# Windowed attention and expert routing on one core: gate products, transposes, quotients and loads of the attention stage in another order

## The chip, the cores and the metric

One core of a Trainium2 chip. The metric is the device time of one execution in microseconds (us); three executions of the kernel before gave 659.93 us as their median (659.71 to 661.52).

## The reference

An attention layer feeds a mixture of experts. Shapes: 8 batches, 8 heads, 576 positions, 64 columns a head; then 4608 tokens of 512 columns, 8 experts, hidden width 1024.

```python
scores = scale * np.matmul(q, k.transpose(0, 1, 3, 2))
mask = (rel >= 0) & (rel < window)              # rel = row - column, window = 64
scores = np.where(mask, scores, -1000000000.0)
attn = np.exp(scores - np.max(scores, axis=-1, keepdims=True))
attn = attn / (np.sum(attn, axis=-1, keepdims=True) + 1e-09)
out = np.matmul(attn, v)
...
logits = x @ w_gate                             # x: the attention's output, 4608 x 512
...                                             # tokens go to experts greedily by logit, 576 to each
h = np.maximum(x[mask] @ w1[e], 0.0)
out[mask] = h @ w2[e]
```

## The kernel before

The program has three stretches one behind the other: attention (to about 158 us of the span), the routing of the first expert (to about 185 us), and the experts' two products with the routing of the next expert beside them. The change touches the attention alone.

**Tiling.** A batch has nine blocks of 64 positions. Because of the window a block needs its own keys and those of the block ahead of it, 128 in all. Two consecutive blocks of the whole run (72 of them) make one *unit*: 36 units of 128 rows, 4.5 to a batch. A unit's eight heads are handled in two *groups* of four (`g` = 0, 1).

**A unit's steps.** TensorE multiplies queries and keys (`qk`, L133) into the score banks `Sp`; VectorE adds the mask, negates, and takes the extreme of each row (L142, eight instructions); GpSimd subtracts it (`sm`, L149, one instruction a group); TensorE transposes the result into a bank `Tp` (`tr`, L155, four a group); ScalarE takes the exponent (L157) into `pt`; TensorE multiplies by the values (`pv`, L176) into `Op`. The operand of values has 73 columns a head: 64 of values, 8 that hold the values' product with the gate's weights, and a column of ones that gives the sum of the row. ScalarE copies that sum out (L206), VectorE inverts it (L207) and multiplies the gate columns (L191, into `l`) and the values (L201, into `x`) by it: the *quotient*, once a group. Every fourth unit VectorE sums `l` over heads (L195), and the first expert's choices are then worked off two small operations a unit. `x` is stored to `xs` in memory (L246).

**Order.** The order on every engine is the order in which the code is written; each engine takes its instructions strictly in that order. In loop step `s` stand `qk(s)` with its scores and subtractions, then `tr(s-1)`, then `pv(s-2)` with its quotients, then whatever a table `at` puts at the step's end.

**Gates.** For each batch, in two *halves* (blocks 0 to 3, and 4 to 8), `gate_mm` (L88) multiplies the transposed values `VT` by the gate's weights into a bank `Tp`, `gate_cp` (ScalarE, L92) copies that to `vs`, `gate_tr` (TensorE, L98) transposes it into another bank `Tp`, and `gate_out` (ScalarE, L104 and L107) copies it into the gate columns of `VO`, the values with positions on partitions. `gate_mm` and `gate_cp` stand at the end of one step, `gate_tr` and `gate_out` at the end of the next. There are two `Tp` buffers, handed out in turn to whatever asks: the two groups of `tr`, `gate_mm`, `gate_tr`. A buffer is written again only when ScalarE has read it. Blocks with an even number need values that straddle two tiles of 128 positions; `even` (ScalarE, L119; VectorE, L117, for the first two) moves two halves of 64 partitions into `VE`. These are called *moves* below, two to a block.

**Loads.** The SyncE queue (SP) issues loads in the order written, and waits in that order for the buffers: three each of `Q`, `K` and `VO`, two of `VT`. Batches 0 and 1 are loaded in two parts before the loop, the others by `load_all` (values transposed, queries and keys, values). Stores lag: up to 16 units of `x` are held until step 29.

```python
put(s, gate_mm, b, *i)
put(s, gate_cp, b, *i)
put(s + 1, gate_tr, b, *i)
put(s + 1, gate_out, b, *i)
...
put(s + 1 + max(0, j - 1), even, b, j, not b and j < 2)
```

Of the kernel before, what the change touches and what calls it, by code (L numbers as in the profile page):

```python
# [9 lines left out]
FT = mybir.dt.float32  # L10
# [16 lines left out]
HOLD = 16  # L27
LOADED = 9 * (B - 3) + 12


def attention(ctx, tc, c, q, k, v, vt, gate, xs, L, choices, setup, counters):

    nc = tc.nc
    wgbd, wg = gate
    ld = ctx.enter_context(tc.tile_pool(name="ld", bufs=2))
    wk = ctx.enter_context(tc.tile_pool(name="wk", bufs=3))
    ps = ctx.enter_context(tc.tile_pool(name="ps", bufs=2, space=PSUM))
    po = ctx.enter_context(tc.tile_pool(name="po", bufs=2, space=PSUM))


    SP = [[ps.tile([128, 2, 128], FT, name=f"Sp{r}{i}", bufs=1) for i in range(2)] for r in range(2)]

    def bank():
        return ps.tile([128, 512], FT, name="Tp")
# [1 line left out]
    z = c["zero"]  # L46
    nc.vector.memset(z, 0.0)

    x = po.tile([128, 4, VW], FT, name="Op")
    for _ in range(WARM):  # L50
        nc.tensor.matmul(x[:, 0:2].rearrange("p h w -> p (h w)")[:, 0:128], z, z, start=True, stop=True)
    masks(tc, c)
    Q, K, VO, VE, VT = {}, {}, {}, {}, {}

# [1 line left out]
    PARTS = ((0, 4), (4, NB))  # L56
    ALL = (0, NB)

    def load_vt(b, i0, i1):
        if not i0:  # L60
            VT[b] = ld.tile([128, HP, S], FT, name="VT")
        nc.sync.dma_start(VT[b][:, :, 64 * i0:64 * i1], vt[b, :, :, 64 * i0:64 * i1].rearrange("h p s -> p h s"))

    def load_qk(b, i0, i1, h=slice(0, HP), q2=nc.sync):
        if not i0 and not h.start:
            Q[b] = ld.tile([128, HP, S], FT, name="Q", bufs=3)
            K[b] = ld.tile([128, HP, S], FT, name="K", bufs=3)
        for q1, t, x in ((nc.sync, Q, q), (q2, K, k)):
            q1.dma_start(t[b][:, h, 64 * i0:64 * i1], x[b, h, :, 64 * i0:64 * i1].rearrange("h p s -> p h s"))

    def load_v(b, i0, i1):
        if not i0:
            VO[b] = ld.tile([128, 5, H, VW], FT, name="VO", bufs=3)
        j0, j1 = i0 // 2, i1 // 2
        nc.sync.dma_start(VO[b][:, j0:j1].rearrange("p j h w -> p j (h w)"),
                          v[b, 128 * j0:128 * j1].rearrange("(j p) w -> p j w", p=128))
        if i1 % 2:
            nc.sync.dma_start(VO[b][0:64, j1].rearrange("p h w -> p (h w)"), v[b, 128 * j1:])
# [39 lines left out]
            else:  # L118
                nc.scalar.activation(*a, AF.Copy)  # L119

    PT_, ST, OP_ = {}, {}, {}

    def qk(m, g):
        Sp = [t[g] for t in SP]
# [42 lines left out]
    def pv(m, g):  # L167
        Op = po.tile([128, 4, VW], FT, name="Op")
        pt = PT_.pop((m, g))
# [4 lines left out]
        for h in range(4):  # L174
            for a in range(2):
                nc.tensor.matmul(Op[64 * a:64 * a + 64, h, :], pt[:, h, 64 * a:64 * a + 64],  # L176
                                 vv[a][:, 4 * g + h, :], start=True, stop=True)
        OP_[m, g] = Op

    def norm(m, g):  # L180

        Op = OP_.pop((m, g))
        r = wk.tile([128, 4], FT, name="r", bufs=4)
        if g == 0:
            XT[0] = wk.tile([128, H, D], FT, name="x", bufs=HOLD + 4)
            if m % 4 == 0:
                XT[1] = wk.tile([128, 4, H, E], FT, name="l", bufs=2)
        x, l = XT[0], XT[1]

        def gates():  # L190
            nc.vector.tensor_tensor(l[:, m % 4, 4 * g:4 * g + 4], Op[:, :, 64:72],  # L191
                                    r[:, :, None].to_broadcast([128, 4, E]), OP.mult)
            if g and m in ends:
                j0 = ends[m]
                nc.vector.tensor_reduce(L[:, j0:m + 1, :], l[:, j0 % 4:m % 4 + 1].rearrange("p i h e -> p i e h"),  # L195
                                        axis=AX.X, op=OP.add)
                if m != 34:
                    late.extend(choices(min(j0, 32), m + 1))

        def values():  # L200
            nc.vector.tensor_tensor(x[:, 4 * g:4 * g + 4], Op[:, :, 0:64],  # L201
                                    r[:, :, None].to_broadcast([128, 4, 64]), OP.mult)
            if g:
                stores.append((m, x))

        nc.scalar.activation(r, Op[:, :, 72], AF.Copy, bias=1e-9)  # L206
        return [lambda: nc.vector.reciprocal(r, r), gates, values]  # L207

    for b in range(2):
        for i in PARTS:  # L210
            if b or i[0]:
                load_qk(b, *i)
            else:
                load_qk(b, *i, slice(0, 2), nc.scalar)
                load_qk(b, *i, slice(2, 4), nc.scalar)
                nc.sync.dma_start(wgbd, wg)
                counters()
            load_vt(b, *i)
            load_v(b, *i)

    def load_all(b):
        load_vt(b, *ALL)
        load_qk(b, *ALL)
        load_v(b, *ALL)

    n = 36
    at = {}

    def put(s, f, *a):
        at.setdefault(s, []).append((f, a))  # L230

    for b in range(B):
# [12 lines left out]
    def store(m, x):  # L245
        nc.sync.dma_start(xs[128 * m:128 * m + 128], x.rearrange("p h d -> p (h d)"))  # L246

    def small(s):
        if late:
            late.pop(0)()  # L250
        if s > 1:
            for _ in range(2 if s < 5 else 1):
                next(setup, None)

    for s in range(n + 2):
# [11 lines left out]
        if 2 <= s:  # L267
            for g in range(2):
                pv(s - 2, g)
            nrm = [norm(s - 2, g) for g in range(2)]  # L270
            for inv, gates, values in nrm:
                for f in (inv, gates, values) if s < n + 1 else (inv, gates):
                    f()
            if s >= n:
                while late:
                    late.pop(0)()
            if s == n + 1:
                for inv, gates, values in nrm:
                    values()
        for f, a in at.get(s, []):  # L280
            f(*a)
        for _ in range(1 if 2 * s < LOADED else 2):
            if stores and (len(stores) > HOLD or 2 * s > LOADED):
                store(*stores.pop(0))
    for m, x in stores:
        store(m, x)
# [68 lines left out]
class Routing:  # L355
# [715 lines left out]
```

## Time and profile before

| | |
|---|---|
| median of 3 executions | 659.93 us (659.71 to 661.52) |
| the profiled execution's own time | 659.36 us |
| its span, first to last instruction | 657.7 us |
| mean granted TensorE clock | 0.974 of full speed |
| busy share: TensorE, its weight loads, VectorE, ScalarE, GpSimd | 95%, 81%, 66%, 51%, 33% |
| HBM read and written | 82.15 MB and 18.87 MB |

The busy shares are means over all three stretches, and matmuls are pipelined, so a busy TensorE need not be one at its peak. In rows of single instructions the first number is the start in us from the start of the span, the second the time of the row; "x8" says that eight like instructions were merged; a bracket gives the idle time of that engine ahead of the row and what ended it. "issue" is time in which the engine waited for nothing that the profile shows. PE is TensorE's matmul, PEld its weight load, DVE VectorE, ACT ScalarE, POOL GpSimd, SPq the SyncE queue.

### The profile page before, as it was taken

The page shows a single profiled execution, that of the slowest core. Times are in us where ns is not written, and L with a number is a line of the kernel's source. Part 1 is how long each engine was busy: PE and PEld are TensorE (multiplying, and loading weights), DVE is VectorE, ACT ScalarE, POOL GpSimd, SP SyncE. Part 2 cuts the span into 40 slices and gives each one's busy share as a digit, 9 for nine tenths or more (in the row PEclk, how much of TensorE's full clock was granted, in tenths as well). Part 3 has the DMA queues.
Part 4 walks back from the last instruction along what each step waited for, and adds up shares of the span by engine and source line. Part 5 has one row for each costly group of instructions (what it writes and reads, how often), then busy time and mean ns, then how long its engine had stood idle before and what let it go on. Part 6 is the DMA issues. An engine that isn't in the chain of part 4 may idle for free. (4 is left out here: it accounts for less than half of the span.)

```text
span 657.7 us, 16919 instructions
## 1 busy us (share of the span) xinstructions
PE 622.0 (95%) x6383; PEld 533.8 (81%) x6383; DVE 433.0 (66%) x2109; ACT 335.6 (51%) x602; POOL 219.2 (33%) x233
## 2 busy tenths in 40 slices
PE   7889999996489999999999999999999999999995
PEld 6667777775379878987997898899789879989984
DVE  5788888887787776875886687588668852202300
ACT  2586777783056157436715642672564266256310
POOL 3644545552051043206303320630342063052211
PEclk8999999998589999999999999999999999999998
DMA  9999989931087279739847972975798299939701
GB/s 302 339 366 375 353 286 377 380 142 67 18 279 154 41 266 232 159 106 268 200 87 259 232 164 94 269 197 102 252 223 182 70 289 257 233 106 215 145 24 48
DMA packets 50097, 134.10 MB, mean 204 GB/s; under 512 B 4696, under 2 KB 10968, under 8 KB 50016
## 3 DMA queue, kind: packets, MB, share of 16 engines
q0 software_dynamic: 15280, 52.98, 36.2%
q1 hardware_dynamic: 34192, 79.52, 33.8%
q8 instruction: 50, 0.82, 0.5%
q10 hardware_dynamic: 544, 0.52, 0.2%
q14 instruction: 31, 0.25, 0.1%
HBM read 82.15 MB, written 18.87 MB: 154 GB/s over the span
## 5 line engine op out<-in xcount | busy, mean ns | idle before, releaser
L951 POOL DMA_INDIRECT out<-ot,idx x40 | 40.8, 1021 | 296.4 <-DVE ab L629 98.4
L900 ACT ACTIVATE hh<-h 128x256 fp32r<-128x256 f32 (+1 forms) x128 | 52.1, 408 | 103.7 <-PE h L928 102.7
L971 PE MATMUL o<-wh,hl 128*128 128x512 f32 x256 | 102.2, 399 | 0.0
L971 PE MATMUL o<-wl,hh 128*128 128x512 f32 x256 | 102.0, 398 | 0.0
L971 PE MATMUL o<-wh,hh 128*128 128x512 f32 x256 | 100.4, 392 | 0.0
L149 POOL TENSOR_TENSOR st<-st,mx 128x512 f32<-128x512 f32 x72 | 73.4, 1040 | 73.7 <-DVE mx L142 54.2
L928 PE MATMUL h<-xh,wl 128*128 128x256 f32 (+1 forms) x512 | 94.4, 299 | 0.0
L928 PE MATMUL h<-xh,wh 128*128 128x256 f32 (+1 forms) x512 | 91.6, 299 | 0.7 <-ACT xh L856 0.7
L928 PE MATMUL h<-xl,wh 128*128 128x256 f32 (+1 forms) x512 | 91.1, 297 | 0.5 <-DVE xl L860 0.5
L905 DVE SCALAR_TENSOR_TENSOR hl<-h,hh 128x256 fp32r<-128x256 f32 x128 | 53.3, 416 | 42.4 <-ACT hh L900 42.0
L928 PEld LDWEIGHTS h<-xh,wh 128*128 128x128 f32 x512 | 75.6, 189 | 1.6 <-ACT xh L856 0.8
L928 PEld LDWEIGHTS h<-xh,wl 128*128 128x128 f32 x512 | 76.4, 189 | 0.2
L928 PEld LDWEIGHTS h<-xl,wh 128*128 128x128 f32 x512 | 75.5, 189 | 0.8 <-DVE xl L860 0.7
L142 DVE CUSTOM_DVE_ANT_0 st<-Sp,mask 128x128 f32<-128x128 f32 x288 | 67.4, 285 | 8.0 <-PE Sp L133 7.7
L811 ACT ACTIVATE wh<-st 128x1024 fp32r<-128x1024 f32 x64 | 67.2, 1050 | 3.3 <-DMA st<-w 3.0
L820 ACT ACTIVATE wl<-wh 128x1024 fp32r<-128x1024 f32 x61 | 64.5, 1057 | 1.2
L822 POOL DMA_DIRECT2D wl<-st x61 | 56.9, 1236 | 17.4 <-ACT wl L820 14.5
L971 PEld LDWEIGHTS o<-wl,hh 128*128 128x128 f32 x256 | 48.1, 188 | 9.3
L971 PEld LDWEIGHTS o<-wh,hh 128*128 128x128 f32 x256 | 48.2, 188 | 9.2
L971 PEld LDWEIGHTS o<-wh,hl 128*128 128x128 f32 x256 | 48.3, 189 | 8.8
L860 DVE TENSOR_TENSOR xl<-tp,xh 128x512 fp32r<-128x512 f32 (+1 forms) x40 | 25.0, 633 | 45.3 <-ACT xh L856 44.9
L866 POOL DMA_INDIRECT xg<-xs,idx x40 | 40.8, 1020 | 34.7 <-DVE eq L709 23.1
(178 smaller groups left out, 1088.4 us busy)
## 6 DMA issues: line engine op xcount, KB each, us to landing
wl<-st POOLq DMA_DIRECT2D x61, 512.0 KB
st<-w SPq DMA_DIRECT2D x60, 512.0 KB, 10.0
xs<-x SPq DMA_DIRECT2D x36, 256.0 KB, 8.0
VO<-v SPq DMA_DIRECT2D x6, 1168.0 KB, 17.8
VT<-vt SPq DMA_DIRECT2D x6, 1152.0 KB, 14.3
Q<-q SPq DMA_DIRECT2D x6, 1152.0 KB
K<-k SPq DMA_DIRECT2D x6, 1152.0 KB
VO<-v SPq DMA_DIRECT2D x4, 584.0 KB, 11.1
```

The lines of the kernel that those rows point to most:

```text
L142: nc.vector.tensor_tensor_reduce(st[:, h, :], Sp[h % 2][:, h // 2], mk, scale=-0.125, scalar=3.0e38, op0=OP.add, op1=OP.min, accum_out=mx[ ...
L149: nc.gpsimd.tensor_tensor(st, st, mx[:, :, None].to_broadcast([128, 4, 128]), OP.subtract)
L811: nc.scalar.activation(hi, st[i], AF.Copy)
L820: nc.scalar.activation(lo, hi.bitcast(FT), AF.Copy, scale=-1.0)
L822: nc.gpsimd.dma_start(lo.bitcast(FT), st[i], accum_op=OP.add)
L860: nc.vector.tensor_tensor(xl[:, :, r], t[:, :, :n], xh[:, :, r].bitcast(FT), OP.subtract)
L866: nc.gpsimd.indirect_dma_start(out=g[0:n, a], out_offset=None, in_=self.xs, in_offset=IndirectOffsetOnAxis(ap=idx[0:n, a:a + 1], axis=0))
L900: nc.scalar.activation(hh[:, f, c0:c1], h, AF.Relu)
L905: nc.vector.scalar_tensor_tensor(t, h[:, a - c0:b - c0], 0.0, hh[:, f, a:b].bitcast(FT), op0=OP.max, op1=OP.subtract)
L928: nc.tensor.matmul(h, wv[:, cc, 128 * (f % 2):128 * (f % 2) + 128], xt[:, cc, c0:c1], start=(k == 0), stop=(k == 11))
L951: nc.gpsimd.indirect_dma_start(out=self.out, out_offset=IndirectOffsetOnAxis(ap=idx[0:m, a:a + 1], axis=0), in_=ot[0:m], in_offset=None)
L971: nc.tensor.matmul(o, ht[:, f, 128 * a:128 * a + 128], wt[:, 512 * (f % 2):512 * (f % 2) + 512], start=(k == 0), stop=(k == 23))
```

## The change

- **Banks.** `Sp` becomes one tile of two banks for each group, `Op` one tile of two banks for both groups, in one copy in place of two of one bank each. The banks in use stay eight.
- **One quotient a unit.** The copy of the sums, the inversion, and the two multiplications each handle both groups: four instructions a unit where there were eight, and they begin when the second group's products are done.
- **Gates.** `gate_tr` and `gate_out` move from the end of the next step to between its `qk` and its `tr`. The moves come at a step's end behind `gate_mm` and `gate_cp`. The halves come in the last step of the batch before and the first of their own (the first two batches and the last have steps of their own).
- **Loads.** Of batch 0, blocks 4 and 5 of queries and keys come ahead of the values; of batches from 2 on, queries and keys, then transposed values, then (a step later) values.
- **The end.** In step 36 the products and quotient of unit 34 stand ahead of the transposes of unit 35, in the banks of the scores' first group.
- `LOADED`, from which two stores are allowed a step, is step 30 in place of 29.

```diff
-LOADED = 9 * (B - 3) + 12
+LOADED = 29
...
-    po = ctx.enter_context(tc.tile_pool(name="po", bufs=2, space=PSUM))
+    po = ctx.enter_context(tc.tile_pool(name="po", bufs=1, space=PSUM))
...
+    SB = [ps.tile([128, 2, 512], FT, name=f"Sp{i}", bufs=1) for i in range(2)]
+    SP = [[x[:, r, 0:256].rearrange("p (h k) -> p h k", h=2) for x in SB] for r in range(2)]
...
+    def pv(m):
+        Ob = SB[0] if m == n - 2 else po.tile([128, 2, 512], FT, name="Op")
+        Op = Ob[:, :, 0:4 * VW].rearrange("p g (h w) -> p g h w", h=4)
...
+        def values():
+            nc.vector.tensor_tensor(x, Op[:, :, :, 0:64], r[:, :, :, None].to_broadcast([128, 2, 4, 64]), OP.mult)
+            stores.append((m, x.rearrange("p g h d -> p (g h d)")))
+
+        nc.scalar.activation(r, Op[:, :, :, 72], AF.Copy, bias=1e-9)
+        return lambda: nc.vector.reciprocal(r, r), gates, values
...
+    load_qk(0, 4, 6)
+    load_vt(0, 0, 4)
+    load_v(0, 0, 4)
+    load_qk(0, 6, NB)
+    load_vt(0, 4, NB)
+    load_v(0, 4, NB)
...
-        s0 = (9 * (b - 1) + (6 if b < 4 else 7)) // 2
-        for i, s in zip(PARTS, ((0, 2), (3, 5))[b] if b < 2 else (s0, s0 + 2)):
+        f = 9 * b // 2
+        for i, s in zip(PARTS, {0: (1, 2), 1: (5, 6), B - 1: (f - 3, f - 1)}.get(b, (f - 1, f))):
             put(s, gate_mm, b, *i)
             put(s, gate_cp, b, *i)
-            put(s + 1, gate_tr, b, *i)
-            put(s + 1, gate_out, b, *i)
+            put(s + 0.5, gate_tr, b, *i)
+            put(s + 0.5, gate_out, b, *i)
             for j in range(4):
                 if i[0] <= 2 * j + 2 < i[1]:
-                    put(s + 1 + max(0, j - 1), even, b, j, not b and j < 2)
+                    put(s + 1.25 + max(0, j - 1), even, b, j, not b and j < 2)
     for b in range(2, B):
-        put((9 * (b - 2) + 5) // 2, load_all, b)
+        f = 9 * b // 2
+        put(f - 7, load_qk, b, *ALL)
+        put(f - 7, load_vt, b, *ALL)
+        put(f - 6, load_v, b, *ALL)
...
+        do(s - 0.5)
+        if s == n:
+            quotients(s)
         if 1 <= s < n + 1:
             for g in range(2):
                 tr(s - 1, g)
...
+        if 2 <= s and s != n:
+            quotients(s)
+        do(s)
+        do(s + 0.25)
```

ScalarE's order around the second half of batch 5, before (`vs` is the copy of a gate product, `VO<-Tp` the copy into the gate columns, `VE` the moves, `pt` the exponents, `r` the sums):

```order
L92 ACTIVATE vs<-Tp 128x320
L157 ACTIVATE pt<-Tp 128x512 x2
L206 ACTIVATE r<-Op 128x4 x2
L104 ACTIVATE VO<-Tp 128x16x8
L107 ACTIVATE VO<-Tp 64x8x8
L119 ACTIVATE VE<-VO 64x584 x2
L157 ACTIVATE pt<-Tp 128x512 x2
```

and with the change:

```order
L93 ACTIVATE vs<-Tp 128x320
L120 ACTIVATE VE<-VO 64x584 x2
L105 ACTIVATE VO<-Tp 128x16x8
L108 ACTIVATE VO<-Tp 64x8x8
L159 ACTIVATE pt<-Tp 128x512 x2
L206 ACTIVATE r<-Op 128x8
```

The copy into the gate columns stood a unit behind the copy of the product, ahead of the moves; now it stands in the same stretch with a pair of moves between the two. Of the sixteen halves, four had moves between the two copies; now twelve have, one of them (second half of batch 2) four instructions.

TensorE's order at the same place, with the change (`Sp` scores, `Tp<-ident,vs` the gate's transposes, `Tp<-ident,st` a unit's eight transposes, `Op` products; before, the gate's transposes stood behind the unit's products, a whole unit's `qk` ahead of the next `Tp<-ident,st`):

```order
L89 MATMUL Tp<-VT,wgs 32x320 x4
L135 MATMUL Sp_95<-K,Q 64x128 x8
L135 MATMUL Sp_96<-K,Q 64x128 x8
L99 MATMUL Tp<-ident,vs 128x128 x2
L99 MATMUL Tp<-ident,vs 64x128
L157 MATMUL Tp<-ident,st 128x128 x8
L180 MATMUL Op<-VE,pt 64x73
```

The gate's transposes now stand directly ahead of a unit's transposes. Since the two `Tp` buffers are handed out in turn, the gate's product and the first group's transposes share one, the gate's transposes and the second group's transposes the other.

## Rows read from the trace of the kernel before

**Rows 1.** Busy time of each engine in two stretches, the attention up to unit 11 and from there to the last scores: us, length, busy us and instructions of PE, PEld, DVE, ACT, POOL, granted clock, DMA share, GB/s.

```profile
5.00:54.00 49.00, 42.40 (x782) 32.49 (x783) 35.73 (x260) 27.19 (x65) 24.10 (x25) 0.97 1.06 359
54.00:147.00 93.00, 90.86 (x1838) 72.05 (x1837) 79.25 (x568) 70.19 (x165) 48.36 (x48) 1.00 0.88 318
```

**Rows 2.** Groups of instructions up to 165 us, shapes apart: line, engine, operation, tiles, shapes, count | busy us, mean ns of one | idle us ahead of them and what ended it.

```profile
L119 ACT ACTIVATE VE<-VO 64x584 f32<-64x584 f32 x60 | 41.3, 689 | 1.3
...
L201 DVE TENSOR_TENSOR x<-Op,r 128x256 f32<-128x256 f32 x72 | 29.8, 415 | 0.2 <-issue 0.2
...
L191 DVE TENSOR_TENSOR l<-Op,r 128x32 f32<-128x32 f32 x72 | 13.8, 192 | 7.5
```

**Rows 3.** Single instructions in order of time, end of unit 18 and unit 19, which has no gate product: scores, transposes, products on PE, the second group's quotient on DVE and the next scores.

```profile
84.71 0.44 PE L98 MATMUL Tp<-ident,vs 128*128 128x128 f32 x2
...
85.08 1.10 PE L133 MATMUL Sp<-K,Q 64*64 64x128 f32 x32
...
85.24 0.17 DVE L207 RECIPROCAL r<-r 128x4 f32<-128x4 f32 x1
...
85.51 0.19 DVE L191 TENSOR_TENSOR l<-Op,r 128x32 f32<-128x32 f32 x1
85.62 0.41 DVE L201 TENSOR_TENSOR x<-Op,r 128x256 f32<-128x256 f32 x1
85.95 0.28 DVE L142 CUSTOM_DVE_ANT_0 st<-Sp,mask 128x128 f32<-128x128 f32 x1
86.11 1.09 PE L155 MATMUL Tp<-ident,st 128*128 128x128 f32 x8
...
87.14 0.28 PE L176 MATMUL Op<-VE,pt 128*64 128x73 f32 x1
```

**Rows 4.** Single instructions of PE and of ACT, one gate half of five blocks: its product, the scores behind it, its transposes; the copy of the product, the two copies into the gate columns; and a pair of moves.

```profile
88.31 0.74 PE L88 MATMUL Tp<-VT,wgs 128*32 128x320 f32 x8
88.99 1.10 PE L133 MATMUL Sp<-K,Q 64*64 64x128 f32 x32
...
92.22 0.55 PE L98 MATMUL Tp<-ident,vs 128*128 128x128 f32 x3
92.70 0.56 PE L133 MATMUL Sp<-K,Q 64*64 64x128 f32 x12
...
85.51 1.39 ACT L119 ACTIVATE VE<-VO 64x584 f32<-64x584 f32 x2
...
89.13 0.44 ACT L92 ACTIVATE vs<-Tp 128x320 f32<-128x320 f32 x1 [0.52 <-PE Tp L88]
...
92.81 0.29 ACT L104 ACTIVATE VO<-Tp 128x128 f32<-128x128 f32 x1 [0.29 <-PE Tp L98]
92.98 0.21 ACT L107 ACTIVATE VO<-Tp 64x64 f32<-64x64 f32 x1
```

**Rows 5.** Weight loads that waited at a `Tp` buffer from 54 to 147 us, from the first to the last of eight (0.20 to 0.32 us each).

```profile
82.95 0.42 PEld L155 LDWEIGHTS Tp<-ident,st 128*128 128x128 f32 x4 [0.22 <-issue]
...
102.07 0.42 PEld L155 LDWEIGHTS Tp<-ident,st 128*128 128x128 f32 x4 [0.32 <-issue]
...
104.05 0.16 PEld L88 LDWEIGHTS Tp<-VT,wgs 128*32 128x32 f32 x8 [0.30 <-ACT pt L157]
...
139.36 0.16 PEld L88 LDWEIGHTS Tp<-VT,wgs 128*32 128x32 f32 x8 [0.30 <-ACT pt L157]
```

**Rows 6.** Weight loads that stood still in the middle of a row of like instructions, with nothing in the profile that they waited for.

```profile
20.80 0.19 PEld L133 LDWEIGHTS Sp<-K,Q 64*64 64x64 f32 x4 [2.15 <-issue]
...
49.45 0.13 PEld L176 LDWEIGHTS Op<-VE,pt 128*64 128x64 f32 x1 [1.10 <-issue]
...
62.68 0.79 PEld L133 LDWEIGHTS Sp<-K,Q 64*64 64x64 f32 x25 [1.08 <-issue]
...
113.18 0.30 PEld L133 LDWEIGHTS Sp<-K,Q 64*64 64x64 f32 x9 [0.88 <-issue]
```

**Rows 7.** The first half of batch 2 at its copy into the gate columns (ACT), and the second group's transposes behind it (PEld).

```profile
46.52 0.29 ACT L104 ACTIVATE VO<-Tp 128x128 f32<-128x128 f32 x1 [0.69 <-DMA VO<-v]
...
46.93 0.42 PEld L155 LDWEIGHTS Tp<-ident,st 128*128 128x128 f32 x4 [0.99 <-issue]
```

**Rows 8.** The attention's end on PE and DVE: the transposes of unit 35, the products of unit 35 (one row for each group) and the last inversion.

```profile
150.90 0.66 PE L155 MATMUL Tp<-ident,st 128*128 128x128 f32 x4 [0.48 <-POOL st L149]
151.89 0.66 PE L155 MATMUL Tp<-ident,st 128*128 128x128 f32 x4 [0.34 <-POOL st L149]
...
154.42 0.25 PE L176 MATMUL Op<-VO,pt 128*64 128x73 f32 x1 [0.69 <-DVE r L207]
155.68 0.25 PE L176 MATMUL Op<-VO,pt 128*64 128x73 f32 x1 [0.52 <-DVE best L452]
...
156.65 0.18 DVE L207 RECIPROCAL r<-r 128x4 f32<-128x4 f32 x1 [0.42 <-ACT r L206]
```

**Rows 9.** Who waited for whom up to 160 us: engine, tile and line, what it waited for, us in total, times, longest.

```profile
PEld Op L176 <- DVE mx L142: 2.7, 16, 0.2
...
PEld Sp L133 <- DVE r L207: 1.9, 4, 0.5
...
PEld Sp L133 <- DVE l L191: 1.8, 7, 0.4
PEld Sp L133 <- DVE x L201: 1.6, 3, 0.5
```

More of the change, by code (lines that the diff above doesn't have):

```diff
@@ L37, in attention @@
     ps = ctx.enter_context(tc.tile_pool(name="ps", bufs=2, space=PSUM))
-    po = ctx.enter_context(tc.tile_pool(name="po", bufs=2, space=PSUM))
-    SP = [[ps.tile([128, 2, 128], FT, name=f"Sp{r}{i}", bufs=1) for i in range(2)] for r in range(2)]
+    po = ctx.enter_context(tc.tile_pool(name="po", bufs=1, space=PSUM))
+    SB = [ps.tile([128, 2, 512], FT, name=f"Sp{i}", bufs=1) for i in range(2)]
+    SP = [[x[:, r, 0:256].rearrange("p (h k) -> p h k", h=2) for x in SB] for r in range(2)]
     def bank():
@@ L47, in attention @@
     nc.vector.memset(z, 0.0)
-    x = po.tile([128, 4, VW], FT, name="Op")
+    x = po.tile([128, 2, 512], FT, name="Op")
     for _ in range(WARM):
-        nc.tensor.matmul(x[:, 0:2].rearrange("p h w -> p (h w)")[:, 0:128], z, z, start=True, stop=True)
+        nc.tensor.matmul(x[:, 0, 0:128], z, z, start=True, stop=True)
     masks(tc, c)
@@ L119, in even @@
                 nc.scalar.activation(*a, AF.Copy)
-    PT_, ST, OP_ = {}, {}, {}
+    PT_, ST = {}, {}
+    n = 36
     def qk(m, g):
@@ L173, in pv, with norm @@
             vv.append(VO[b][:, i // 2] if (i % 2 or i == 0) else VE[b][:, i // 2 - 1])
[L174 to L188, printed above, removed]
+        for g in range(2):
+            pt = PT_.pop((m, g))
+            for h in range(4):
+                for a in range(2):
+                    nc.tensor.matmul(Op[64 * a:64 * a + 64, g, h, :], pt[:, h, 64 * a:64 * a + 64],
+                                     vv[a][:, 4 * g + h, :], start=True, stop=True)
+        return Op
+    def norm(m, Op):
+        r = wk.tile([128, 2, 4], FT, name="r", bufs=2)
+        x = wk.tile([128, 2, 4, D], FT, name="x", bufs=HOLD + 4)
+        if m % 4 == 0:
+            XT[1] = wk.tile([128, 4, H, E], FT, name="l", bufs=2)
+        l = XT[1]
         def gates():
-            nc.vector.tensor_tensor(l[:, m % 4, 4 * g:4 * g + 4], Op[:, :, 64:72],
-                                    r[:, :, None].to_broadcast([128, 4, E]), OP.mult)
-            if g and m in ends:
+            nc.vector.tensor_tensor(l[:, m % 4].rearrange("p (g h) e -> p g h e", g=2), Op[:, :, :, 64:72],
+                                    r[:, :, :, None].to_broadcast([128, 2, 4, E]), OP.mult)
+            if m in ends:
                 j0 = ends[m]
@@ L200, in values @@
         def values():
[L201 to L226, printed above, removed]
+            nc.vector.tensor_tensor(x, Op[:, :, :, 0:64], r[:, :, :, None].to_broadcast([128, 2, 4, 64]), OP.mult)
+            stores.append((m, x.rearrange("p g h d -> p (g h d)")))
+        nc.scalar.activation(r, Op[:, :, :, 72], AF.Copy, bias=1e-9)
+        return lambda: nc.vector.reciprocal(r, r), gates, values
+    load_qk(0, 0, 4, slice(0, 2), nc.scalar)
+    load_qk(0, 0, 4, slice(2, 4), nc.scalar)
+    nc.sync.dma_start(wgbd, wg)
+    counters()
+    load_qk(0, 4, 6)
[4 more added lines that the diff above has]
+    load_v(0, 4, NB)
+    for i in PARTS:
+        load_qk(1, *i)
+        load_vt(1, *i)
+        load_v(1, *i)
     at = {}
@@ L230, in put, with do @@
         at.setdefault(s, []).append((f, a))
+    def do(s):
+        for f, a in at.get(s, []):
+            f(*a)
     for b in range(B):
-        s0 = (9 * (b - 1) + (6 if b < 4 else 7)) // 2
-        for i, s in zip(PARTS, ((0, 2), (3, 5))[b] if b < 2 else (s0, s0 + 2)):
+        f = 9 * b // 2
+        for i, s in zip(PARTS, {0: (1, 2), 1: (5, 6), B - 1: (f - 3, f - 1)}.get(b, (f - 1, f))):
             put(s, gate_mm, b, *i)
             put(s, gate_cp, b, *i)
-            put(s + 1, gate_tr, b, *i)
-            put(s + 1, gate_out, b, *i)
+            put(s + 0.5, gate_tr, b, *i)
+            put(s + 0.5, gate_out, b, *i)
             for j in range(4):
                 if i[0] <= 2 * j + 2 < i[1]:
-                    put(s + 1 + max(0, j - 1), even, b, j, not b and j < 2)
+                    put(s + 1.25 + max(0, j - 1), even, b, j, not b and j < 2)
     for b in range(2, B):
-        put((9 * (b - 2) + 5) // 2, load_all, b)
+        f = 9 * b // 2
+        put(f - 7, load_qk, b, *ALL)
+        put(f - 7, load_vt, b, *ALL)
+        put(f - 6, load_v, b, *ALL)
     def store(m, x):
-        nc.sync.dma_start(xs[128 * m:128 * m + 128], x.rearrange("p h d -> p (h d)"))
+        nc.sync.dma_start(xs[128 * m:128 * m + 128], x)
     def small(s):
@@ L253, in small, with quotients @@
                 next(setup, None)
+    def quotients(s):
+        inv, gates, values = norm(s - 2, pv(s - 2))
+        for f in (inv, gates, values) if s < n + 1 else (inv, gates):
+            f()
+        if s >= n:
+            while late:
+                late.pop(0)()
+        if s == n + 1:
+            values()
     for s in range(n + 2):
@@ L266, in attention @@
                 tr(s - 1, g)
[L267 to L283, printed above, removed]
+        if 2 <= s and s != n:
+            quotients(s)
+        do(s)
+        do(s + 0.25)
+        for _ in range(1 if s < LOADED else 2):
+            if stores and (len(stores) > HOLD or s > LOADED):
                 store(*stores.pop(0))
```

3 lines of the change are left out of this document (removed).

## The prediction

> **What bounds the kernel now.** Start with the busy time by stretch [rows 1]. From unit 11 to the last scores TensorE shows 90.86 us busy of 93.00, at a granted clock of 1.00 (the 2.4 GHz level); before that 42.40 of 49.00, with a DMA share of 1.06. So the attention is first limited by loads, then by TensorE. A busy matmul row can hide small waits, so look next at single instructions. A unit without gate work [rows 3]: scores start at 85.08, transposes at 86.11, products at 87.14, and what follows at 88.31 [rows 4]: 1.03 + 1.03 + 1.17 = 3.23 us with nothing free in it. Gate work comes on top: 0.68 us for a product of five blocks (88.31 to 88.99) and 0.48 for its transposes (92.22 to 92.70) [rows 4], 0.37 for the transposes of four blocks (84.71 to 85.08) [rows 3]. A reader should see that only three sorts of time can be won: loads up to unit 10, waits at TensorE, and the end. The chain at the kernel's end lies far behind; routing and experts are not touched, so I let a microsecond at the attention's end count as one at the kernel's end.
>
> **One quotient a unit: 0 us.** On DVE the second group's inversion starts at 85.24, its multiplication of values at 85.62, the next scores at 85.95 [rows 3]: 0.71 us a group, 1.4 for two. Joined, inversion to values is about the same 0.4, and a multiplication of 512 columns is longer than one of 256 by 256 columns; taking the slope between the 192 ns for 32 columns and the 415 for 256 [rows 2], 1.0 ns a column, that is 0.33 + 0.26 = 0.59. So 1.0 us a unit, 0.4 less, 15 us over 36 units. None of it is on the path: DVE is busy 79.25 of 93.00 [rows 1] and the next scores banks are read long before TensorE wants them. What covers it is TensorE's 3.23 us; without that cover up to 15 us could be won. The other side: `Op` is now one buffer. The sums can be copied about 0.3 us after the last product, so the quotient ends some 1.2 + 0.3 + 0.2 + 0.4 + 0.7 = 2.8 us after the unit's products start; the next products start 3.23 after. Each fourth unit adds a reduction over heads of about 0.6 and may wait 0.1 to 0.2: at most 1 us in all. I take 0 between −8.0 (all waits put down to DVE, below) and +0.9.
>
> The Trainium skill, "Perfetto Trace Analysis", section "Optimizing Tensor Performance", says that independent groups of matmuls should rotate through PSUM banks so that one is emptied while the next runs; this change gives up that rotation for `Op`. By the rule the products would wait in every unit; by rows 3 they come 0.4 us after the bank is free.
>
> **Gates between scores and transposes: +6.2 us of new waits, −2.1 of old ones.** The gate's transposes and the second group's transposes share a `Tp` buffer, so the second group waits until ScalarE has copied the gate's transposes out. Before, a unit's scores and first group (1.03 + 0.5) lay between. Now only the first group's 0.5 does, and on ScalarE a pair of moves stands ahead of the copy. Count from the start of a five-block product [rows 4]. TensorE: 0.68 + 1.03 (scores) + 0.48 (gate transposes) + 0.50 (first group) = 2.69. ScalarE: the copy of the product starts after 0.82 (88.31 to 89.13) and takes 0.44; the moves take 1.39, the two copies 0.38 (92.81 to 93.19), and 0.12 passes to TensorE (46.52 + 0.29 to 46.93 [rows 7]): 3.15. The second group waits 0.46. Four blocks are shorter on both sides: about the same. With no moves between, the copy ends about when it is wanted: 0 to 0.1. With four moves (second half of batch 2) two more of 0.69 [rows 2]: 1.85.
>
> Eleven halves have one pair. Three of them (batch 1, and the first half of batch 2) come before the point where loads decide, below, and are free. Left: 8 × 0.46 = 3.7, the one of 1.85, 0.1 for the two halves without moves, and about 0.5 where batch 7's first product comes behind four moves in one step and an exponent it needs is late: 6.2. Off come the eight waits of 0.20 to 0.32 of the old order in this stretch, 2.1 [rows 5]. Net +4.1; bounds +1.5 (waits half as long) and +5.
>
> **Loads in order of need: 0 us at the kernel's end.** The first gate product no longer stands ahead of unit 1, and unit 2's keys come ahead of the values, so units 1 to 8 start some 2 us earlier. It doesn't last. The first half of batch 2 cannot be copied into `VO` before that batch's values are there: before, ScalarE waited 0.69 us for just this load until 46.52, and TensorE 0.99 behind it [rows 7]. By then all of batches 0 to 2 has been loaded, 3 × 4.9 = 14.7 MB. At the 359 GB/s of a saturated DMA [rows 1] that is 41 us after the first loads, in either order, and this load is last in both. So both kernels leave unit 9 at the same time. Bounds: 0 and −2 (if the queue gains on it). The issue steps of later batches don't matter: SP runs ahead of the units and waits for buffers alone.
>
> **The end: −1.8 us.** At 150.3 TensorE has nothing but to wait for GpSimd (0.48 and 0.34), then unit 35's products wait 0.69 for the bank of unit 34's quotient and 0.52 for the second [rows 8]. With unit 34's products put into the first gap, the second group's transposes still start at about 152.0, its exponent ends near 153.4, the products end at 154.0, the last inversion starts near 154.45 instead of 156.65: −2.2. Least: the two waits themselves, −1.2. I take −1.8.
>
> **Code loading: −0.4 us.** Four times weight loads stand still for 0.88 to 2.15 us amid like instructions with nothing to wait for [rows 6], while DMA is busy. I take this as late instruction packets. The number of TensorE's instructions is unchanged, so I expect as many; one may fall into a wait that is there anyway. Bounds: −3.1 (the three after 46 us gone) and +1.1 (one more).
>
> **Sum.** 4.1 + 0 + 0 − 1.8 − 0.4 = +1.9. The profiled execution took 659.36 (a span of 657.7 and 1.7 around it), so 661.3; the median of the runs is 0.57 above it: **661.8 us**. About 0.3%, 2 us, is what a measurement of this kernel can tell from no change, and the forecast lies on that edge.
>
> **Rivals.**
> - *DVE sets the pace* (faster). If the scores of a unit start late because the quotient ahead of them is long, TensorE waits for it, and joining the quotients pays. The waits of TensorE put down to DVE come to 2.7 + 1.9 + 1.8 + 1.6 = 8.0 us [rows 9]. All gone: 661.8 − 8.0 = 653.8. It decides if DVE ends last where TensorE waits for a scores bank. Against it: each is 0.17 to 0.5 us, just what stands as "issue" at the same places, the change from one sort of matmul to the next. The Trainium skill, "Perfetto Trace Analysis", section "Optimizing Scalar/DVE Operations", says that joining small operations helps where the engine is saturated; its 125 ns for an access to PSUM, for three instructions a unit, would make an estimated 13 us. Chance 0.09.
> - *New waits swallow the code loading* (no change). If instruction packets catch up in the twelve new waits, the three late ones after 46 us vanish: 661.8 + 0.4 − 3.1 = 659.1. Chance 0.30. If the second group's waits are also half as long, 656.5: chance 0.05.
> - *The early lead holds* (no change). If batch 2's values land 2 us earlier: 659.8. For it: the next batches' buffers are free sooner. Against it: DMA share 1.06. Chance 0.06.
> - *The single `Op` buffer bites as well* (slower): +0.9, and one more late packet, +1.5: 664.2. Chance 0.06.
>
> **How the numbers follow.** The forecast itself has 0.44. Its likely result scatters across the 2 us edge by the bounds above, but mostly to slower. With the last rival, slower 0.50; faster 0.09 + 0.05 = 0.14; the rest, 0.36, within. The range leaves out the DVE rival and the outer bounds: low 657.2 (the swallowed packets with an end of −2.2, and waits a little shorter), high 664.8 (the forecast with an end of −1.2, the `Op` waits and a late packet).
>
> **What would show it.** Right: the second group's transposes behind gate transposes wait 0.4 to 0.5 us, and near 2 us once, near 52 us; scores of unit 1 start about 2 us earlier, those of unit 10 no earlier, those of unit 35 some 4 us later than 146.99; from there to the last inversion 7.5 to 8.5 us where 9.66 were. Wrong: units of 3.0 us or less, which would make DVE the bound; no idle time at the second group's transposes; unit 10 two microseconds ahead.

## The result, and the profile after

| | before | after |
|---|---|---|
| median | 659.83 us (659.58 to 661.57, 6 runs) | 663.94 us (662.91 to 664.37, 6 runs) |
| ratio, 95% interval | | 1.0053 [1.0039, 1.0066] |
| profiled execution, its span | 659.36, 657.7 us | 663.08, 661.4 us |
| scores of unit 10 start | 50.59 | 49.20 |
| scores of unit 35 start | 146.99 | 153.70 |
| last inversion | 156.65 | 161.41 |

Slower, by 0.5% (the medians alone give 1.0062). Read the difference of the two profiles along the span: 1.39 us ahead at unit 10; from there to unit 35 104.50 us in place of 96.40, 8.10 lost; from unit 35 to the last inversion 7.71 in place of 9.66, 1.95 won; another 1.0 is won behind the attention (below). Together 3.7 us.

The stretch from unit 11 to the last scores, with the columns of [rows 1], and the joined multiplication of values by its group over the attention:

```profile
54.80:153.70 98.90, 91.20 (x1838) 72.78 (x1834) 72.61 (x493) 69.63 (x143) 47.04 (x47) 1.00 0.82 294
```
```profile
L203 DVE TENSOR_TENSOR x<-Op,r 128x512 f32<-128x512 f32 x33 | 22.5, 682 | 0.0
```

As many matmuls as in [rows 1], the same busy time (91.20 against 90.86), the clock at 1.00: the 5.9 us more are idle time of TensorE. DVE fell from 79.25 us busy (of 93.00) to 72.61 (of 98.90).

Now one gate half of five blocks, the counterpart of [rows 3, 4]: product, its copy, the pair of moves, scores, gate transposes, first group, the two copies, second group; and below the half of batch 2 with four moves.

```profile
88.15 0.74 PE L89 MATMUL Tp<-VT,wgs 128*32 128x320 f32 x8
...
88.83 1.10 PE L135 MATMUL Sp<-K,Q 64*64 64x128 f32 x32
...
88.97 0.44 ACT L93 ACTIVATE vs<-Tp 128x320 f32<-128x320 f32 x1 [0.52 <-PE Tp L89]
...
89.43 1.39 ACT L120 ACTIVATE VE<-VO 64x584 f32<-64x584 f32 x2
...
89.86 0.55 PE L99 MATMUL Tp<-ident,vs 128*128 128x128 f32 x3
...
90.25 0.60 PE L157 MATMUL Tp<-ident,st 128*128 128x128 f32 x4
...
90.84 0.29 ACT L105 ACTIVATE VO<-Tp 128x128 f32<-128x128 f32 x1
...
91.02 0.21 ACT L108 ACTIVATE VO<-Tp 64x64 f32<-64x64 f32 x1
...
91.30 0.42 PEld L157 LDWEIGHTS Tp<-ident,st 128*128 128x128 f32 x4 [0.69 <-issue]
```
```profile
53.08 0.42 PEld L157 LDWEIGHTS Tp<-ident,st 128*128 128x128 f32 x4 [2.10 <-POOL st L151]
```

ScalarE has no gap from 88.97 to the end of the copies: 0.82 + 0.44 + 1.39 + 0.38 + 0.12 = 3.15 us from the product's start to the second group, to the hundredth what was forecast. TensorE is there after 2.46, not 2.69: the gate's transposes followed by like transposes take 0.39 where they took 0.48 ahead of scores, and the weight loads of the first group are through in 0.36, not 0.50. Ten halves wait 0.68 to 0.70 in this way, one 2.10. The releaser printed (issue, POOL) is the last event that the profile saw, not the cause: GpSimd's result was long there.

The stalls amid a row of like instructions, the counterpart of [rows 6]:

```profile
63.33 0.41 PEld L135 LDWEIGHTS Sp<-K,Q 64*64 64x64 f32 x13 [1.15 <-issue]
...
77.96 0.19 PEld L135 LDWEIGHTS Sp<-K,Q 64*64 64x64 f32 x3 [1.46 <-issue]
...
98.51 0.20 PEld L135 LDWEIGHTS Sp<-K,Q 64*64 64x64 f32 x7 [1.06 <-issue]
...
118.40 0.30 PEld L135 LDWEIGHTS Sp<-K,Q 64*64 64x64 f32 x10 [0.56 <-issue]
```

With two smaller ones (0.41 at 71.44, 0.23 at 92.31) 4.87 us from unit 10 on; before it was 1.08 + 0.28 + 0.88 = 2.24 (stalls of 0.2 us and more are counted, here and below).

The trace's records of DMA show what ends them. TensorE's next instructions come as packets of 16 KB (queue 8, kind "instruction"). The packets ahead of the four stalls shown end at 61.79, 76.56, 97.06 and 116.95, and TensorE goes on 1.40 to 1.54 us later; those ahead of the three of before end at 61.36, 67.85 and 111.67, and TensorE goes on 1.32 to 1.51 us later. So it is with every stall counted in the kernels below: it ends 1.27 to 1.58 us behind the end of such a packet. The stalls fall on the same weight loads of the program each time, about 126 or a multiple of it apart. Call them *places*: to go on there TensorE needs the next packet.

And the end, for [rows 8]: unit 34's products now lie ahead of unit 35's second group, and the waits of 0.69 and 0.52 have become one of 0.31.

```profile
155.70 0.42 PEld L157 LDWEIGHTS Tp<-ident,st 128*128 128x128 f32 x4 [0.35 <-POOL st L151]
...
159.90 0.28 PE L180 MATMUL Op<-VO,pt 128*64 128x73 f32 x1 [0.31 <-ACT pt L159]
...
161.41 0.20 DVE L207 RECIPROCAL r<-r 128x8 f32<-128x8 f32 x1 [0.59 <-ACT r L206]
```

### The profile page after: what moved, and what is told of

Read it like the earlier page. It is cut to its first block, busy times and chain, and to the rows that moved or that the text cites. A ratio compares the mean times of both kernels' runs of the same rounds, so it can differ in the third digit from the quotient of the medians.

```text
span 661.4 us, 16743 instructions
## 1 busy us (share of the span) xinstructions
PE 619.7 (94%) x6383; PEld 533.1 (81%) x6383; DVE 423.4 (64%) x2001; ACT 331.9 (50%) x566; POOL 219.6 (33%) x233
```

## The experiments

Two theories. **W**: the waits at the shared `Tp` buffer cost what they last. **C**: TensorE loses time at late instruction packets, and a wait only covers what would be lost there anyway. Times are medians; ratios are to runs of the kernel before on the same chip, so compare by ratios. The kernels without loads or moves leave that work out.

| kernel | us | ratio, 95% interval | unit 10 to 35, us |
|---|---|---|---|
| before | 659.83 | | 96.40 |
| changed | 663.94 | 1.0053 [1.0039, 1.0066] | 104.50 |
| changed, second profile | 663.43 | 1.0070 [1.0050, 1.0090] | 104.60 |
| gates' transposes back | 659.51 | 0.9996 [0.9978, 1.0014] | 99.72 |
| moves first | 664.90 | 1.0082 [1.0064, 1.0100] | 104.33 |
| changed, no loads | 658.02 | 0.9980 [0.9966, 0.9994] | 99.32 |
| before, no loads | 656.06 | 0.9947 [0.9928, 0.9966] | 94.27 |
| quotient only | 660.25 | 1.0013 [0.9999, 1.0027] | 97.12 |
| old gate steps | 661.79 | 1.0035 [1.0019, 1.0052] | 98.94 |
| moves on DVE | 667.04 | 1.0125 [1.0105, 1.0145] | 107.44 |
| old loads | 663.63 | 1.0064 [1.0048, 1.0081] | 103.54 |
| quotient and end | 657.25 | 0.9974 [0.9958, 0.9989] | 97.22 |
| no moves | 660.11 | 1.0018 [1.0002, 1.0034] | 101.31 |
| gate transposes in `Op` | 658.36 | 0.9993 [0.9978, 1.0009] | 99.12 |

**1. The pair without loads.** In both kernels, and likewise for `VT` and `VO`:

```diff
+        if b > 1:
+            Q[b], K[b] = Q[b - 2], K[b - 2]
+            return
...
```

> The changed kernel without the loads of batches 2 to 7: they take the Q, K, V and gate inputs of batch b-2 in their place (the output differs by that); every engine instruction stays. With e4_before_noload this takes the DMA traffic away from under the units. Theory W with late packets behind a saturated DMA: no stalls amid rows of over .3 us after 35 us, the second group's waits of .5 to .7 stay, the scores of unit 35 some 3 to 4 us later than in the kernel before with the same cut, and the whole 1 to 2.5 us slower than it. Theory C: the pair differs by under .5 us. Theory D (stalls have nothing to do with DMA): four to eight of .4 to 1.5 us remain.

> The kernel before with the same loads left out (batches 2 to 7 take the inputs of batch b-2; the output differs by that). Packets behind a saturated DMA: the stalls amid rows after 35 us (1.10, 1.08, .28 and .88 in the kernel before) vanish, the waits of .2 to .3 for the Tp buffer stay, unit 10 starts at 44 to 47 in place of 50.6, time 650 to 655. Theory D: the stalls remain and only the start of unit 10 moves.

First the changed kernel, then the one before (line numbers are 9 higher): DMA's share from 52 to 142 us (last but one column), unit 10's and unit 35's scores, and in the changed one the two sorts of wait.

```profile
52.00:142.00 90.00, 85.20 (x1757) 68.45 (x1757) 67.11 (x460) 66.38 (x139) 45.55 (x46) 1.00 0.18 67
...
48.41 0.78 PE L144 MATMUL Sp<-K,Q 64*64 64x128 f32 x20
...
52.28 0.42 PEld L166 LDWEIGHTS Tp<-ident,st 128*128 128x128 f32 x4 [2.09 <-POOL st L160]
...
87.34 0.42 PEld L166 LDWEIGHTS Tp<-ident,st 128*128 128x128 f32 x4 [0.69 <-issue]
...
147.73 0.67 PE L144 MATMUL Sp<-K,Q 64*64 64x128 f32 x16
```
```profile
52.00:142.00 90.00, 89.42 (x1812) 70.77 (x1814) 78.50 (x567) 69.82 (x163) 48.88 (x48) 1.00 0.19 71
...
48.63 0.56 PE L142 MATMUL Sp<-K,Q 64*64 64x128 f32 x12
...
142.90 0.56 PE L142 MATMUL Sp<-K,Q 64*64 64x128 f32 x12
```

After 35 us no stall of the kind of [rows 6] is left in either, though both run the same instructions; so these stalls hang on DMA. The waits for `Tp` stay; in the changed kernel one half more waits 0.69 in place of 0.24, since the stall of 1.15 at 63.33, which had given ScalarE the time, is gone. (I had the kernel before at unit 10 by 47 us and done in 655; with 48.63 and 656.06 less of the first part depends on the later loads than I thought.) From unit 10 to 35 the pair shows what the change costs without stalls: 99.32 − 94.27 = 5.05 us. The joined quotient is in it as well, but adds nothing to this stretch (experiment 6), so I call it the gates' part. Unit 35 starts 4.8 us later, where W had 3 to 4. With the end the pair differs by 1.96, inside W's 1 to 2.5; C's "under 0.5" falls. With loads the same stretch costs the kernel before 2.13 more, the changed kernel 5.18 more: the late packets' part is 3.05.

**2. Gates' transposes back, from batch 2 on,** with their copy and the moves on the same step:

```diff
-            put(s + 0.5, gate_tr, b, *i)
+            put(s + (1 if b > 1 else 0.5), gate_tr, b, *i)
...
```

> The changed kernel, but from batch 2 on the gate's transposes, their copy and the moves stand again at the end of the next unit (one unit after the gate's product), as before the change; one quotient, order of loads and end stay. Theory W (the waits of the second group's transposes for the shared Tp buffer cost the time, and every microsecond of them arrives at the end): the eleven waits of .69 and the one of 2.10 us vanish, eight of .2 to .3 come back, last inversion 154.5 to 156.5 where the changed kernel has 161.2, time 658 to 659.5 us. Theory C (the loss is late instruction packets, and the new waits only cover what would be lost at packets anyway): the Tp waits vanish but stalls amid a row of like matmuls grow by as much, time 662 to 664.

The long waits are gone (0.22 to 0.42 is left), and the last inversion is at 157.43, a microsecond later than W had it. The time is at the upper edge of what W gave; by ratios 0.6% come back, all that the change had lost. But the end's 2 us don't show as a gain: this kernel still has a batch's two halves one unit apart, and needs 99.72 us from unit 10 to 35, where the kernel before needs 96.40. So it does not isolate the step. The second kernel has the halves' old steps as well:

```diff
-        f = 9 * b // 2
-        for i, s in zip(PARTS, {0: (1, 2), 1: (5, 6), B - 1: (f - 3, f - 1)}.get(b, (f - 1, f))):
+        s0 = (9 * (b - 1) + (6 if b < 4 else 7)) // 2
+        for i, s in zip(PARTS, {0: (1, 2), 1: (5, 6)}.get(b, (s0, s0 + 2))):
...
```

> The changed kernel with the gate work of batches 2 to 7 on the very steps it had before the change (the kernel with the gates' transposes put back still had the two halves of a batch one unit apart where two lay between before). One quotient, order of loads and end stay. Theory W: from unit 10 to unit 35 as long as in the kernel before (96.4 us, of which some 2 are late packets), last inversion 7.5 us after the scores of unit 35: time 656.5 to 658.5, faster than both. Theory C (whatever is saved comes back as late packets): 659 to 661.

A miss, of both theories: 661.79. The reason stands in the first gate product of batch 2 on its old step, its weight load and its matmul:

```profile
43.03 0.19 PEld L89 LDWEIGHTS Tp<-VT,wgs 128*32 128x32 f32 x8 [3.38 <-issue]
43.07 0.64 PE L89 MATMUL Tp<-VT,wgs 128*32 128x256 f32 x8 [3.26 <-DMA VT<-vt]
```

The new order of loads brings `VT` behind `Q` and `K`, and the old step asks for it too early: unit 10 starts at 53.97. Steps of the gates and order of loads are a pair. Its stalls are 4.3 us, so the old gate steps with the new loads didn't bring back the 2.24 of before. Less its stalls its stretch from unit 10 to 35 takes 94.7 us; so reckoned the kernel before takes 94.2 and the changed one 99.6. On the old steps the gates' part is gone.

**3. Order of loads alone** (the first two batches as before, too)**, and the changed kernel again.**

```diff
...
-        put(f - 7, load_qk, b, *ALL)
-        put(f - 7, load_vt, b, *ALL)
-        put(f - 6, load_v, b, *ALL)
+        put((9 * (b - 2) + 5) // 2, load_all, b)
```

> The changed kernel with the loads in the order and at the steps of the kernel before; gate steps, quotient and end as changed. My term for the order of loads is 0: unit 1 starts 2 us later, unit 10 within 0.5 us of the changed kernel's 49.2, time 663 to 665. If the order of loads is what put more late packets behind the units (4.9 us of stalls amid rows after unit 10, 2.2 before), the stalls fall to 2 to 3 and the time to 661 to 662.5. If the early lead is worth what it is at unit 1: 665.5 to 666.5.

> The changed kernel once more, for a second profile on this chip. If the late packets are fixed by how the kernel's loads and instructions fall together: stalls amid rows after unit 10 of 4 to 5.5 us, as in the first profile, at the same instructions, time 663 to 665. If they are chance: 2 to 6 us, at other instructions.

With the old order unit 10 starts at 51.04, 1.8 us later than in the changed kernel, where I had 0.5, and yet the time is the same: 663.63 beside 663.43. The stalls behind unit 10 are 4.0 us in place of 4.8. In the second profile of the changed kernel the stalls stand at the same instructions, 4.84 us in all; two of them:

```profile
77.65 0.19 PEld L135 LDWEIGHTS Sp<-K,Q 64*64 64x64 f32 x3 [1.45 <-issue]
...
98.75 0.20 PEld L135 LDWEIGHTS Sp<-K,Q 64*64 64x64 f32 x7 [1.61 <-issue]
```

They are not chance: this kernel's loads and instructions fall together so in both profiles.

**4. What holds the second group.** Three edits: the moves from batch 1 on ahead of the gate product's copy; the moves on DVE; the gate's transposes (`gate_tr`) in the products' banks.

```diff
-                    put(s + 1.25 + max(0, j - 1), even, b, j, not b and j < 2)
+                    put(s + 0.75 + max(0, j - 1) + (0 if b else 0.5), even, b, j, not b and j < 2)
...
+        do(s - 0.25)
         do(s)
```
```diff
-                    put(s + 1.25 + max(0, j - 1), even, b, j, not b and j < 2)
+                    put(s + 1.25 + max(0, j - 1), even, b, j, True)
```
```diff
-        pt = VS[b][0] = bank()
+        pt = VS[b][0] = po.tile([128, 2, 512], FT, name="Op")[:, 0]
```

> The changed kernel with one edit: the moves are issued at the unit's end ahead of the next gate product's copy, not between that copy and the copy of the gate's transposes. Gate transposes stay between scores and transposes. Theory W: the second group's wait shrinks from .69 to 0.1 to 0.3 us, the one of 2.10 by 1 to 1.4, but the copy of the gate's product starts .6 us later and part of the wait moves to the gate's transposes (0 to .4 each); time 659.5 to 662, between the changed kernel and the one with the gates put back. Theory C: the same 662.5 to 664, with more stalls amid rows.

> The changed kernel with the moves from VO to VE on DVE (0.52 us each, as the four that are there already) in place of ScalarE (0.69). Order of everything else as in the changed kernel. If the moves on ScalarE between the copy of the gate's product and the copy of its transposes make the second group wait, the eleven waits fall to 0.3 or less and the one of 2.10 too: time 656.5 to 660. Rival (DVE has no room: some 2.9 us of its own in a unit and 1.04 of moves): scores are read late in the units with moves, scores matmuls wait 0.3 to 1 us, 661 to 665.

> The changed kernel with the gate's transposes in the products' banks (Op) in place of a Tp buffer; order of the instructions unchanged. If it is the shared Tp buffer that makes the second group wait: its waits fall to 0 to .2; the unit's products now wait for ScalarE's copy instead, which comes .5 us later in the row (0 to .3), and the gate's transposes may wait for the quotient before (0 to .4): time 658 to 661.5. If the second group waits for something else: .69 stays and the time is 664 or more.

The same half in the three kernels, of the second its total of waits from 48 to 160 us (engine, tile and line, what it waited for, us, times, longest) and its busy time in the changed kernel's stretch instead:

```profile
90.65 0.28 PEld L99 LDWEIGHTS Tp<-ident,vs 128*128 128x128 f32 x3 [0.69 <-ACT vs L93]
...
91.69 0.42 PEld L157 LDWEIGHTS Tp<-ident,st 128*128 128x128 f32 x4 [0.29 <-issue]
```
```profile
PEld Sp L135 <- DVE mx L144: 12.1, 27, 1.7
...
54.80:153.70 98.90, 92.67 (x1779) 69.62 (x1780) 92.39 (x522) 38.76 (x94) 47.65 (x48) 1.00 0.81 292
```
```profile
87.96 0.28 PEld L99 LDWEIGHTS Op<-ident,vs 128*128 128x128 f32 x3 [0.17 <-issue]
88.24 0.91 PEld L157 LDWEIGHTS Tp<-ident,st 128*128 128x128 f32 x8
89.38 0.13 PEld L180 LDWEIGHTS Op<-VO,pt 128*64 128x64 f32 x1 [0.23 <-ACT VO L108]
```

Moves first: the wait moves to the gate's own transposes, where I had at most 0.4 and it takes 0.69, and 0.29 stays: no faster than the changed kernel (104.33 beside 104.50 and 104.60 from unit 10 to 35; the ratios' intervals overlap). Moves on DVE: the long waits are gone and DVE, now 92.39 busy of 98.90, makes the scores' banks late, 12.1 us in 27 waits (0.7 in two in the changed kernel); the rival won, by more than it said. Its stalls come to 0.86 us: a TensorE that comes later to a place finds the packet there. Transposes in `Op`: eight transposes of both groups in one row with no wait, the products 0.23 later. Elsewhere the gate's transposes wait up to 0.81, twice what I had, and behind four moves the products wait 1.12, where I had 0.3 at most, but the kernel is 5 us faster than the changed one, with the order untouched. So it is the shared buffer that holds the second group, and the moves on ScalarE that keep the buffer.

**5. The moves left out,** with `VE[b - 2]` in place of `VE[b]`:

```diff
     def even(b, j, early):
 
+        if b > 1:
+            return
```

> The changed kernel without the moves from batch 2 on (the pairs that straddle take the first batches' moved values in their place, so the output differs). ScalarE's chain from the gate's product to the copy of its transposes loses 1.39 us of 3.15. Theory W: all the waits of .69 and the one of 2.10 at the second group's transposes fall to .24 (what the kernel shows without moves between), that is 9 times .45 and 1.86, 5.9 us from unit 10 on, and the time to 657 to 659. Theory C (late packets take the saved time back): stalls amid rows of over 6 us after unit 10 where 4.9 were, time 661 to 663.5.

Between the two: 660.11. The waits fell as W says, from unit 10 on seven of 0.69 to 0.24 or 0.29 and the one of 2.10 to 0.69, and the stalls grew as C says, to 6.36 us. Compare the two stalls of the same instructions (the line is 2 higher) with the changed kernel's above:

```profile
77.50 0.19 PEld L137 LDWEIGHTS Sp<-K,Q 64*64 64x64 f32 x3 [1.73 <-issue]
...
98.47 0.20 PEld L137 LDWEIGHTS Sp<-K,Q 64*64 64x64 f32 x7 [1.34 <-issue]
```

At the first the kernel without moves arrives 0.73 us earlier and leaves 0.46 earlier; at the second it arrives 0.32 earlier and leaves 0.04 earlier. TensorE goes on when the packet is there: the packets end at 76.07 (without moves) and 76.56, at 97.00 and 97.06, and it goes on 1.4 to 1.5 us behind each. A lead is worth only what the packet comes earlier. What is saved behind 98.5 (five waits of about 0.4, and 0.42 at the product of batch 7) stays: the last inversion comes 2.5 us earlier.

**6. The quotient alone, and the quotient with the end.** The kernel before with `SB`, `pv(m)`, `norm(m, Op)` and the single `Op` of the change; then with these lines too, the second ahead of the last transposes:

```diff
...
+        Ob = SB[0] if m == n - 2 else po.tile([128, 2, 512], FT, name="Op")
...
+        if s == n:
+            quotients(s)
```

> The kernel before with one part of the change alone: one quotient a unit, with its two-bank layout of scores and products and its single Op buffer. Gate steps, loads and end as before. My term: no change in the units, but at the end the last products wait for the one Op buffer until unit 34's quotient is done, 0.5 to 1 us more than the two waits of 0.69 and 0.52 of before: last inversion 0 to 1 us later, time 659.3 to 661. Rival Q (the single buffer costs in every unit): 33 waits of 0.1 us or more at the products, 662 or more. Rival P (DVE sets the pace, so fewer quotients pay): 653 to 657.

> The kernel with one quotient alone (660.25 us), and the end of the change with it: unit 34's products ahead of the last transposes, into the scores' banks. Gate steps and loads as in the kernel before. If the end is a term of its own: the wait of 2.18 us at the last products falls to about 0.5, last scores to last inversion 6.2 us (DVE's scores of unit 35 to the inversion) where the quotient alone shows 8.8, time 657 to 658.5, faster than both kernels by 0.2 to 0.4 per cent against before. Theory C (savings come back as late packets): not here, since no load is left at the end; it would need 659.5 to 661.

The last products' wait and the last inversion, first with the quotient alone, then with the end:

```profile
155.59 0.13 PEld L180 LDWEIGHTS Op<-VO,pt 128*64 128x64 f32 x1 [2.18 <-issue]
...
157.12 0.20 DVE L207 RECIPROCAL r<-r 128x8 f32<-128x8 f32 x1 [1.32 <-ACT r L206]
```
```profile
152.71 0.13 PEld L180 LDWEIGHTS Op<-VO,pt 128*64 128x64 f32 x1 [0.58 <-ACT pt L159]
...
154.22 0.20 DVE L207 RECIPROCAL r<-r 128x8 f32<-128x8 f32 x1
```

Both as I had them. From unit 10 to 35 the quotient takes 0.72 us more than the kernel before, with 0.86 more of stalls; so it costs nothing but 0.5 us at the end; the end gives 2.6 us on top of it by the ratios, 2.7 by the traces (from unit 35's scores to the last inversion 7.47 in place of 10.16). This kernel, with the gates and loads of before, is the fastest of those that leave no work out: 657.25 us, 0.9974 [0.9958, 0.9989], by the ratio 1.7 us under the kernel before.

## Why the prediction held, and the term that was wrong

Slower, and inside the range, but 2.1 us above the forecast. Of what was to show it: scores of unit 1 start at 7.12, 2.3 us earlier; the second group waits 0.69 and once 2.10; unit 35 starts 6.7 us later than 146.99, not 4; and from there to the last inversion it takes 7.71. By its terms:

- **One quotient, 0**: right. DVE's quotient takes 0.20 + 0.22 + 0.68 us; the estimate of 0.59 for the values was low by 0.09, without effect. The products start 0.17 us later than usual in two units (0.34 at 137.28, 0.35 at 152.49), which also shows without loads; alone the quotient costs +0.5 at the end.
- **Gates, +4.1 (1.5 to 5)**: the mechanism and ScalarE's 3.15 us were right. New waits from unit 10 on came to 8.1, not 6.2, because TensorE arrives 0.23 earlier. Less the old waits of 2.1, and less 0.1 for each of eleven rows of gate transposes, which are that much shorter than before, that makes 4.9. Measured without loads: +5.05, just over the upper bound.
- **Loads, 0**: right for the time, as near as these runs tell (experiment 3). As to how, half right: in the second profile ScalarE waits until 46.55 us for batch 2's values, where it was 46.52 before [rows 7], but unit 10 still starts 1.2 to 1.4 earlier; 1.10 of that is a late packet that the kernel before meets at 49.45 [rows 6]. Most of the lead goes at the next packets, not at this load.
- **End, −1.8 (−1.2 to −2.2)**: right, −1.95.
- **Code loading, −0.4 (−3.1 to +1.1)**: this is the step that failed. The forecast took as many late packets because the count of instructions is the same, and put the range's other end at one more. There were six stalls in place of three: +2.6 by their rows, +3.05 by the pair without loads.
- Behind the attention, not in the sum: −1.0 in the profile. From the last inversion to the end it takes 501.1 us before and 500.0 after, and between 499.7 and 501.8 in the other kernels, whose code there is the same. I take it as scatter.

5.05 + 3.05 − 1.4 − 1.95 − 1.0 = 3.75, where the profiles differ by 3.7. The rival in which new waits swallow the code loading had a link that the runs show: less waiting can bring more stalls (6.36 us without the moves, 4.87 with them), and more waiting fewer (0.86 with the moves on DVE). It is no rule: with the gate transposes in `Op` there is less waiting and 4.2 us of stalls. And the rival missed that the packets themselves begin later: the changed kernel has more of both than the kernel before. That the time still fell inside the range owes something to luck: the gates cost 0.95 more than forecast and the packets 3.45 more, and the 1.4 of lead at unit 10 and the 1.0 of scatter, neither of them forecast, took 2.4 off again.

**Why the packets were late.** Whether a packet is late depends not on how many there are but on when it begins, and on how soon TensorE comes to the next place. Without loads 25 of 28 begin within 1 us of TensorE's passing the place before (places without a stall are counted on from those with one, about 126 weight loads each). Behind the places passed from 62 to 93 us the next packet begins 0.25 to 4.05 us later in the kernel before, and 3.9 to 5.5 us in the changed one, where DMA is fuller (share in the last but one column, first before, then changed):

```profile
62.00:93.00 31.00, 30.18 (x616) 24.29 (x619) 26.39 (x189) 21.48 (x53) 16.60 (x17) 1.00 0.88 314
...
62.00:93.00 31.00, 27.51 (x532) 21.57 (x530) 21.34 (x144) 20.11 (x42) 15.44 (x16) 1.00 1.05 375
```

**DVE sets the pace** fell: units without gate work still take 3.23 us with DVE at 72.61 of 98.90. The Trainium skill, "Perfetto Trace Analysis", section "Optimizing Scalar/DVE Operations", ties the gain of joined operations to a saturated engine. The trace agrees as far as it goes: nothing was won here with DVE at 72.61 of 98.90; no run joins operations on a saturated one. (The prediction's estimate of 13 us by that section counts the inversion as an access to PSUM, but it reads and writes `r`, which lies in SBUF; the two multiplications alone would make an estimated 9.)

What stays open: which loads the changed kernel's packets stand behind. The DMA share from 62 to 93 us does not settle it alone: with the old order of loads the changed kernel shows 0.85 there and 4.0 us of stalls all the same. Between the kernels with loads the sum differs from 0.86 (moves on DVE) to 6.36 (no moves). No run here moved the packets themselves.

## What to carry to other kernels

Before you move a step between two others that share a rotating buffer, lay the chain of the engine that frees the buffer beside the chain of the one that wants it, from a common start, with everything queued on the first: here 3.15 against 2.46 us. A wait then moves easily and seldom vanishes: ahead of the copy it fell on the gate's transposes, on DVE on the scores, and in another bank it nearly went. And where loads saturate DMA for the whole stage, a lead won in the middle may be lost at the next instruction packet; value it at what comes after the last of them.

## What the runs showed of the hardware that I had not expected

- Instruction packets share DMA with the loads. With a DMA share of 0.80 to 0.88 from unit 11 to the last scores TensorE stood still for 0.9 to 6.4 us in sum from unit 10 on, 0.2 to 1.7 at a time; at 0.18 to 0.19 not at all.
- Such a stall ends 1.27 to 1.58 us behind the end of a 16 KB packet, whenever TensorE came to the place: the changed kernel came to one at 97.45 and 97.14 in its two profiles and left at 98.51 and 98.75; with the moves first it came at 97.85 and left at 98.09.
- Three gate transposes take TensorE 0.39 us ahead of like transposes and 0.48 ahead of scores.
